# Quarter loads shared between two DMA queues, and two GpSimd products moved within a step, in an mLSTM cell followed by a leaky-ReLU feed-forward

## The chip, the cores and the metric

The kernel runs on one core of one Trainium2 chip. The metric is the device time of one execution in microseconds (us), taken as the median of several runs. A profile is taken of one further execution; its span counts from the first to the last instruction and is a little shorter than that execution's own time.

Engines are written as the profile writes them: PE (matrix multiplications; PEld is its weight load), DVE (VectorE), ACT (ScalarE), POOL (GpSimd) and SP (SyncE, which here only issues DMAs). SPq and ACTq are DMA issues by SP and by ACT. DVE, ACT, POOL and PE run their instructions in the order of the program.

## The reference

```python
# q, k, v, o_gate: (4, 8, 768, 40); i_gate, f_gate: (4, 8, 768), all float32
for t in range(S):
    m_new = np.maximum(f_gate[:, :, t] + m, i_gate[:, :, t])
    f_stab = np.exp(f_gate[:, :, t] + m - m_new)
    i_stab = np.exp(i_gate[:, :, t] - m_new)
    m = m_new
    C = f_stab[:, :, None, None] * C + i_stab[:, :, None, None] * np.einsum('bhd,bhe->bhde', vt, kt)
    n = f_stab[:, :, None] * n + i_stab[:, :, None] * kt
    h_tilde = np.einsum('bhde,bhe->bhd', C, qt)
    denom = np.maximum(np.abs(np.einsum('bhd,bhd->bh', n, qt)[:, :, None]), 1.0)
    y[:, :, t] = sigmoid(o_gate[:, :, t]) * h_tilde / denom
x = y.transpose(0, 2, 1, 3).reshape(3072, 320)
h = x @ w_in                                 # w_in: (320, 2048)
out = np.maximum(0.01 * h, h) @ w_out        # w_out: (2048, 320)
```

The two weight matrices arrive as 64-bit floats.

## The kernel before

**Steps and chunks.** The 768 tokens are cut into six chunks c of 128. A step s = 4c + b is one batch b's 128 tokens of chunk c with all eight heads, so there are 24 steps. Chunk 0 (steps 0 to 3) is written out by hand in `first_chunk`. From chunk 1 on a step works on two halves of 64 tokens and carries a state from half to half.

**The feed-forward beside it.** The loop at the end (L1319 on) runs, for each c from 1 to 6, the feed-forward of chunk c-1 as a row of `ffs` units, and puts the cell work of chunk c between the units. PE, DVE, ACT and POOL are filled by hand in this order; the list `place` says after which unit each cell unit comes in chunk 1. There the units are sixteen input products (`half`, L872, 256 columns of tokens each), then sixteen quarters of output products (`part`, L894). The cell units of chunk 1 are, for each step, `u_parts` then `u_plain`.

**A step of chunk 1.** `u_parts(s)` transposes the scaled q (`split_qs`, PE L623, copies on ACT L626), computes the scores inside each half (PE L725) and, mixed with them, the sums that carry the state (PE L731, from the decayed k and from v), multiplies the scores with the decays (DVE L742) and adds to the state (DVE L705, `state_add(s, 0)`). `u_plain(s)` multiplies the mixed q with the state and values (PE L785, tile hN), scales the state for the next half on POOL (L701, `state_next(s, 1)`), normalizes on DVE (L749 to L793), finishes x on POOL (L798, L799) and adds to the state (DVE L705, `state_add(s, 1)`).

**What is prepared ahead.** After `u_plain(s)` the loop calls `ahead(s + 1)`: transposes of k and q (PE L638, ACT L644), exponentials on ACT (L547), then on POOL the scaled q (`prep_qs`, L576, tile y), the state times its decay (`state_next(s+1, 0)`, L701), the decayed k (`prep_vu`, L567, tile vu, called `ku`), and the causal mask of the step after that (`prep_mask(s + 2)`, L537). Before `u_parts(s)` POOL also copies a step's v into place (`split_v`, L416). `ahead(4)` and `split_v(4)` to `split_v(7)` are called at units 3, 5, 9 and 11.

**The weights.** w_in is loaded in four quarters n of 512 columns. A quarter has a lower half r = 0 (256 columns, partitions 0 to 63) and an upper half r = 1 (256 columns, partitions 64 to 127); each of the two holds all 320 rows as five slots of 64. For the quarters 1 to 3 (`WHOLE`) the lower half is one DMA of 640 KB; the upper half is two, of 512 KB and 128 KB, because its slots are rotated (`SLOTS`). All three DMAs of a quarter are issued by SP, one after the other, with rows of 2048 bytes in 64 partitions. The 64-bit words land in a raw area and are narrowed to 32 bits by two ACT and four DVE instructions for each half e of a quarter (`narrow_weights`, L302 to L311), in the order set by `run(now, pace[i])`. The products of quarter n need its two halves e narrowed.

**The queues.** SP's DMAs keep the order in which the program calls `Ordered.dma_start` (L95) as long as `order["on"]` holds, that is through the first chunk and the list at L1283 to L1303: quarter 1 of w_in; the rewritten gates (L360) and the q of step 4; quarter 2; k, v and decays of step 4 (`feed`); quarter 3; then the loads of step 5 around the first part of w_out; steps 6 and 7 around the next parts. The q of step 6 follows behind the part of w_out at L1303. In the first 80 us ACT issues only five small loads of gates.

**The place of the loads.** In `first_chunk` ACT's program order around L1260 is: exponentials and copies of steps 2 and 3, `prep_o(2)` and `prep_o(3)` (ACT L583), then the activation of the next feed-forward unit (L880), the copies of x of steps 2 and 3 (L861, L862) and the narrowing of quarter 1 (`n0`, `n1`).

Of the kernel before, what the change touches and what calls it, by code (L numbers as in the profile page):

```python
# [18 lines left out]
def kernel(  # L19
# [26 lines left out]
    nc = tc.nc  # L46
    B, H, S, D = q.shape
# [3 lines left out]
    NS = B * NB  # L51
# [49 lines left out]
    sync, by_act = queues = Ordered(nc.sync), Ordered(nc.scalar)  # L101
# [20 lines left out]
    for u in range(2):  # L122
        part = ident[ts(u, SL), ts(u, SL)]
        nc.gpsimd.affine_select(
            part, part, compare_op=ALU.not_equal, fill=1.0, base=0, pattern=[[-1, SL]], channel_multiplier=1,
# [109 lines left out]

    WHOLE = (1, 2, 3)

    def load_weights(n, es=(0, 1)):

        m = n - QN  # L240
        if n < QN:
            dst = w_in[:, n, :]
        else:
            dst = w_out[:, 2 * m : 2 * m + 2, :].rearrange("p a d -> p (a d)")
        to = dst
        if wide:
            if n < 2:
                at = NF * GT - 2 * WC * (n + 1)
                raw = acts_l[:, at : at + 2 * WC].bitcast(U64)
            elif n < QN:  # L250
                raw = raw_t[:, WC * (n - 2) : WC * (n - 1)]
            elif m < 2:
                raw = w_out[:].rearrange("p f d -> p (f d)")[:, (2 + m) * WC : (3 + m) * WC].bitcast(U64)
            else:
                at = (4, 0, 1, 2, 3, 4)[m - 2] * HW
                raw = raw_t[:, at : at + HW]
            raws[n] = (raw, dst)
            to = raw
        if n < QN:
            src = moe_w_in[:, n * QC : (n + 1) * QC].rearrange("(k p) (r c) -> r p k c", p=DP, r=2)  # L260
            halves = to.rearrange("p (e k c) -> p e k c", e=2, k=KC)
            both = to.rearrange("p (k c) -> p k c", k=KC)
            if n in WHOLE:
                es = es[:1] if es[0] == 0 else ()
            for e in es:
                for r in range(2):
                    at = 0
                    while at < KC:
                        k0, n_k = run_of(r, at)
                        if n in WHOLE:  # L270
                            rows, part = both[DP * r : DP * (r + 1), at : at + n_k], src[r, :, k0 : k0 + n_k, :]
                        else:
                            rows, part = halves[DP * r : DP * (r + 1), e, at : at + n_k], src[r, :, k0 : k0 + n_k, ts(e, P)]
                        sync.dma_start(rows, part)
                        at += n_k
        else:
            rows = moe_w_out[2 * m * P : 2 * (m + 1) * P, :]
            sync.dma_start(to.rearrange("p (a d) -> p a d", d=Dm), rows.rearrange("(a p) d -> p a d", p=P))
# [270 lines left out]
    def prep_vu(s):  # L549

        c, b = divmod(s, B)
        d = st[s]
        if s < NS:
            d["vu"] = wk.tile([P, H, 2, V1], F32, name="vu")
            g = gT[c][:, 1, ts(b, H)].unsqueeze(2).unsqueeze(3)
            if c == 0:
                nc.gpsimd.tensor_tensor(
                    d["vu"][:, :, :, :DB], d["va"][:, :, :D].rearrange("p h (k d) -> p h k d", d=DB),
                    g.to_broadcast([P, H, 2, DB]), op=ALU.mult,
                )  # L560
                nc.gpsimd.tensor_tensor(
                    d["vu"][:, :, :, DB], d["va"][:, :, D : D + 2], gT[c][:, 1, ts(b, H)].unsqueeze(2).to_broadcast([P, H, 2]),
                    op=ALU.mult,
                )
            else:
                d["ku"] = d["vu"][:].rearrange("p h k d -> p (h k d)")[:, : H * D].rearrange("p (h d) -> p h d", d=D)
                nc.gpsimd.tensor_tensor(  # L567
                    d["ku"], d["k"][:, :, :D], gT[c][:, 1, ts(b, H)].unsqueeze(2).to_broadcast([P, H, D]), op=ALU.mult,
                )

    def prep_qs(s):

        c, b = divmod(s, B)
        d = st[s]
        d["qs"] = wk.tile([P, Dm], F32, name="y")[:].rearrange("p (h d) -> p h d", d=D)
        nc.gpsimd.tensor_tensor(  # L576
            d["qs"], natural(s, 1), gT[c][:, 2, ts(b, H)].unsqueeze(2).to_broadcast([P, H, D]), op=ALU.mult,
        )

    def prep_o(s):  # L580

        o = st[s]["o"] if s < B else natural(s, 2) if s < 2 * B else raw_blocks(s, 2, DB)
        nc.scalar.activation(o, o, AF.Tanh, scale=0.5)  # L583
# [169 lines left out]
    def u_values(s):  # L753
        d = st[s]
        pool, tag = (psc, "c") if s < 2 else (psf, "mm")
        pa = d["pa"] = pool.tile([P, H, D1], F32, name="pa", tag=tag)
        for h in range(H):
            for u in range(2):
                toks = ts(u, SL)
                nc.tensor.matmul(pa[toks, h, :], lhsT=d["w"][:, h, toks], rhs=d["va"][:, h, :D1], start=True, stop=True)  # L760
# [354 lines left out]
    def u_gates(c):  # L1115
        gates_T(c, bus.pop(c)[0])
# [67 lines left out]
    def first_chunk():  # L1184

        for n in range(2):
            for i in range(3):
                load_first(n, i)
        for n in range(2):
            load_first(n, 3)  # L1190
        load_weights(0, (0,))
        on_v, on_s = nc.vector.tensor_copy, nc.scalar.copy
        gates(0)
        gates_exp(0)
        load_fi(2)
        idle(3)
        ab = spread_masks()
        bu, a, _ = bus[0]
        a, left = replicate(a, bu)
        u_transpose(0, (on_v, on_v))  # L1200
        gates(1)
        spread_first(ab, a, left, 0)
        gates_T(0, bu)
        prep_vu(0)
        first_exps(ab, 0)
        u_scores(0)
        u_transpose(1, (on_s, on_s))
        prep_vu(1)
        prepare_tiles()
        u_values(0)  # L1210
        u_scores(1)
        ab = spread_masks()
        spread_first(ab, a, None, 2)
        e = next_exps(ab, 2)
        w, w1 = narrow_weights(0, 0), narrow_weights(0, 1)
        n0, n1 = narrow_weights(1, 0), narrow_weights(1, 1)
        prep_o(0)
        prep_o(1)
        gate(0)
        u_values(1)  # L1220
        load_first(2, 0)
        load_first(2, 1)
        load_weights(0, (1,))
        load_first(3, 0)
        load_first(3, 1)
        load_first(2, 2)
        load_first(3, 2)
        load_first(2, 3)
        load_first(3, 3)
        load_weights(1, (0,))  # L1230
        load_weights(1, (1,))
        run(e, 6)
        state(0)
        state(1)
        run(w, 2)
        u_x(0)
        gate(1)
        run(w, 4)
        u_x(1)
        state_copy(0)  # L1240
        state_copy(1)
        prepare_step(0)
        prepare_step(1)
        run(e, 2)
        ffs = ff_units(0)
        u_transpose(2, (on_s, on_s))
        run(e, 4)
        gates_exp(1)
        run(w1, 2)
        run(e, 4)  # L1250
        ffs[0]()
        run(w1, 2)
        prep_vu(2)
        prep_vu(3)
        u_scores(2)
        u_transpose(3, (on_v, on_s))
        run(w1, 2)
        u_gates(1)
        u_scores(3)
        prep_o(2)  # L1260
        prep_o(3)
        u_values(2)
        ffs[1]()
        gate(2)
        u_values(3)
        gate(3)
        u_x(2)
        state(2)
        u_x(3)
        state(3)  # L1270
        state_copy(2)
        run(n0, 4)
        state_copy(3)
        run(n0, 2)
        run(n1, 6)
        prepare_step(2)
        prepare_step(3)
        return ffs

    E = mybir.EngineType  # L1280
    with tc.manual_schedule(engines={E.PE, E.DVE, E.Activation, E.Pool}):
# [37 lines left out]
        for c in range(1, NB + 1):  # L1319
# [7 lines left out]
            def visits(i):  # L1327
                nonlocal done
                at = place if c == 1 else first_pairs if c == 2 else pairs
                while done < min(n_c, sum(p <= i for p in at)):  # L1330
                    fn, s = cells[done]
                    fn(s)
                    done += 1
                    if fn is u_mix:
                        waiting.append(s)
                    if fn is u_plain and s < 2 * B - 1 or fn is u_parts and s == 2 * B - 1:
                        ahead(s + 1)
                    elif fn is u_mix:
                        after.append(s + 2)
                    elif fn is u_plain:  # L1340
                        prep_mask(s + 2)
                        ahead(s + 2)

            for i in range(n_ff):
# [50 lines left out]
                while fed < done:  # L1395
                    fn, s = cells[fed]
# [42 lines left out]
```

## Time and profile before

| | us |
|---|---|
| median of 3 runs | 473.57 (472.79 to 474.94) |
| the profiled execution | 473.84 |
| its span | 472.0 |
| PE busy within the span | 463.1 |
| PE busy from 0 to 38 us | 33.97 of 38 |
| PE busy from 38 to 85 us | 45.02 of 47 |
| PE busy from 85 to 472 us | 384.08 of 387 |

The profile's timeline lists instructions by start (us from the span's start), duration, engine, line, operation, output and inputs; runs of the same instruction are merged with their count (x8). A bracket at the end tells the idle time of the engine before the instruction and what ended it. The list of waits has, for each pair of waiting and releasing work, us in total, how often, and the longest. The table of stretches gives for each stretch its length, the busy time of each engine with the number of instructions in it, the granted PE clock (1.00 everywhere), the mean busy share of the DMA engines and the rate that they moved.

From 0 to 38 us the kernel is the hand-written first chunk; from 38 to 85 us the input products of chunk 0 run beside steps 4, 5 and 6; from 85 us on one chunk follows the other. The DMA engines are above 90 % busy through most of the first 70 us (a mean share of 1.10 from 0 to 38 us and 0.93 from 38 to 85 us) and half busy after.

### The profile page before, as it was taken

The numbers are of one execution on the slowest core, as the hardware profiler recorded it, in microseconds if no ns is written. First come the engines' busy times: TensorE is split into PE (matmuls) and PEld (weight loads), VectorE is DVE, ScalarE is ACT, GpSimd is POOL, SyncE is SP. The second block draws the span as 40 slices with busy tenths as digits, with TensorE's granted clock in tenths as the row PEclk, the third lists the DMA queues.
The fourth block names the chain that finished last, engine by engine and source line by source line (L and its number), as shares of the span: only waits on it lengthen the run. The fifth ranks groups of instructions, "written<-read, shape, count | busy, mean of one in ns | idle before, by whom it ended". The sixth has DMA issues, their size and how long they took to land.

```text
span 472.0 us, 14167 instructions
## 1 busy us (share of the span) xinstructions
PE 463.1 (98%) x5716; PEld 416.3 (88%) x5716; DVE 336.8 (71%) x609; ACT 203.4 (43%) x497; POOL 171.7 (36%) x225
## 2 busy tenths in 40 slices
PE   9899999999999999999999999999999999999997
PEld 6677978777788999988999988999988999988997
DVE  5778688999479988867788867788847786104541
ACT  2657878755336511366311366311456311253210
POOL 4332377264335164923214923214822005300020
PEclk9999999999999999999999999999999999999999
DMA  9999998887732695865754865853875202100001
GB/s 130 169 192 187 188 205 220 206 181 145 153 110 65 159 166 112 176 153 129 171 119 106 181 130 126 198 114 79 188 151 124 74 9 81 58 0 2 8 8 42
DMA packets 160993, 59.21 MB, mean 125 GB/s; under 512 B 123808, under 2 KB 152352, under 8 KB 160928
## 3 DMA queue, kind: packets, MB, share of 16 engines
q1 hardware_dynamic: 120944, 51.15, 48.9%
q10 hardware_dynamic: 39984, 7.17, 9.4%
q8 instruction: 45, 0.74, 0.7%
q14 instruction: 20, 0.16, 0.1%
HBM read 51.58 MB, written 6.70 MB: 123 GB/s over the span
## 4 chain that ended last, share of the span: by engine, by line
PE 87%; SPq 5%; POOL 3%; issue 3%; DVE 1%; DMA 1%; ACT 0%; POOLq 0%
PE ph L1036 33%; PE po L929 33%; PE po L894 8%; SPq L95 5%; PE pT L813 3%; PE ph L872 3%; PE sd L725 3%; PE sd L731 1%; DMA raw<-in_o_gate_dram 1%; PE hN L785 1%; POOL w L537 1%; POOL y L576 1%; POOL S L701 1%; PE pa L760 0%; PE tk L638 0%
## 5 line engine op out<-in xcount | busy, mean ns | idle before, releaser
L929 PE MATMUL po<-w_out,acts 128*128 128x160 f32 x640 | 89.1, 300 | 0.0
L929 PEld LDWEIGHTS po<-w_out,acts 128*128 128x128 f32 x640 | 87.3, 190 | 0.6 <-ACT acts L1061 0.3
L1036 PE MATMUL ph<-xT,w_in 64*128 64x256 f32 x720 | 82.7, 378 | 0.0
L1036 PEld LDWEIGHTS ph<-xT,w_in 64*128 64x128 f32 x720 | 69.2, 187 | 8.6 <-issue 0.6
L1065 DVE TENSOR_TENSOR acts<-acts,ph 128x512 f32<-128x512 f32 x60 | 38.4, 683 | 40.7 <-PE ph L1036 40.6
L929 PE MATMUL po<-raw,acts 128*128 128x160 f32 x480 | 66.4, 300 | 0.0
L929 PEld LDWEIGHTS po<-raw,acts 128*128 128x128 f32 x480 | 65.4, 190 | 0.3
L537 POOL TENSOR_SCALAR_AFFINE_SELECT w<-w 64x512 f32<-64x512 f32 x40 | 34.0, 850 | 52.9 <-DMA w<-a_dr 51.7
L1069 ACT COPY acts<-ph 128x512 f32<-128x512 f32 x60 | 32.2, 588 | 48.8 <-PE ph L1036 48.8
L1061 ACT ACTIVATE acts<-acts 128x1024 f32<-128x1024 f32 x30 | 31.6, 1055 | 41.8 <-DVE acts L1065 32.4
L701 POOL TENSOR_TENSOR S<-S,f 40x336 f32<-40x336 f32 x36 | 30.6, 849 | 47.8 <-PE pT L813 32.1
L547 ACT ACTIVATE w<-w,gT 128x64 f32<-128x64 f32 x160 | 41.6, 337 | 11.7 <-DMA a_dr<-a 4.3
L742 DVE TENSOR_TENSOR qn<-w,sd 64x384 f32<-64x384 f32 (+1 forms) x80 | 33.4, 418 | 14.3 <-ACT acts L1069 8.4
L872 PE MATMUL ph<-xT,w_in 64*128 64x256 f32 x320 | 37.3, 381 | 0.9 <-issue 0.7
L894 PE MATMUL po<-w_out,acts 128*128 128x320 f32 x128 | 36.7, 437 | 0.0
L1036 PE MATMUL ph<-acts,w 64*128 64x256 f32 x320 | 36.3, 379 | 0.0
L827 POOL TENSOR_TENSOR xb<-xb,den 128x320 f32<-128x320 f32 x16 | 11.6, 727 | 67.0 <-DVE xb L824 64.7
L872 PEld LDWEIGHTS ph<-xT,w_in 64*128 64x128 f32 x320 | 31.9, 187 | 3.8 <-ACT w_out L303 0.9
L1036 PEld LDWEIGHTS ph<-acts,w 64*128 64x128 f32 x320 | 30.6, 187 | 3.6
L894 PEld LDWEIGHTS po<-w_out,acts 128*128 128x128 f32 x128 | 23.5, 190 | 9.2 <-ACT acts L880 0.3
L967 POOL TENSOR_TENSOR y<-y,raw 128x160 f32<-128x160 f32 x10 | 9.5, 950 | 59.5 <-ACT y L966 59.5
L612 DVE TENSOR_TENSOR qn<-kqT,ea 64x512 f32<-64x512 f32 x32 | 30.0, 939 | 0.8
(184 smaller groups left out, 732.2 us busy)
## 6 DMA issues: line engine op xcount, KB each, us to landing
rb<-in_k_dram SPq DMA_DIRECT2D x64, 80.0 KB
rb<-in_q_dram SPq DMA_DIRECT2D x64, 80.0 KB
rb<-in_o_gate_dram SPq DMA_DIRECT2D x64, 80.0 KB
ea<-a_dr SPq DMA_DIRECT2D x32, 128.0 KB
raw<-in_moe_w_out_dram SPq DMA_DIRECT2D x6, 640.0 KB
w<-a_dr ACTq DMA_DIRECT2D x24, 128.0 KB
x_dr<-x SPq DMA_DIRECT2D x64, 40.0 KB
xT<-x_dr SPq DMA_DIRECT2D x16, 160.0 KB
```

The source lines that it names most:

```text
L537: nc.gpsimd.affine_select(part, part, compare_op=ALU.is_ge, fill=-1e30, base=0, pattern=[[0, H], [1, SL]], channel_multiplier=-1,)
L547: yield nc.scalar.activation(w[:, h, :], w[:, h, :], AF.Exp, bias=gT[c][:, 0, bh : bh + 1], scale=1.0)
L612: nc.vector.tensor_tensor(mixed(s)[rows, 1 - r], d["kqT"][rows, 1].rearrange("p (h t) -> p h t", t=SL), d["ea"][rows], op=ALU.mult,)
L701: nc.gpsimd.tensor_tensor(new, old, g, op=ALU.mult)
L742: nc.vector.tensor_tensor(mixed(s)[toks, u, hs], w[toks, hs], bank[1 - u][to[u][hs.start], hs], op=ALU.mult,)
L872: nc.tensor.matmul(ph[r][:, cols], lhsT=w_row(r, slot, j), rhs=xT[DP * r : DP * (r + 1), slot, cols], start=(slot == 0), stop=(slot == KC ...
L894: nc.tensor.matmul(po[n][:], lhsT=acts[:, f, ts(n, P)], rhs=w_out[:, f, :], start=(f == 0), stop=(f == NF - 1),)
L929: nc.tensor.matmul(bank[:], lhsT=left[:, f, :], rhs=right[:, f, :], start=f == 0, stop=f == KH - 1)
L1036: nc.tensor.matmul(bank[r][:, e, :], lhsT=left(r)[rows, e], rhs=right(r)[rows], start=first and e == 0 and m == 0, stop=e == 1 and m == le ...
L1061: nc.scalar.activation(to, z, AF.Prelu, alpha=0.01)
L1065: nc.vector.tensor_tensor(to[:, 2 * r : 2 * r + 2], to[:, 2 * r : 2 * r + 2], bank[r], op=ALU.add)
L1069: nc.scalar.copy(to[:, 2 * r : 2 * r + 2], bank[r])
```

## The change

The change has two parts.

*Loads.* `load_weights` takes the halves r to load as `rs`. Without `rs`, quarters 1 to 3 load only their lower half, on SP as before. A new call in `first_chunk`, between `prep_o(3)` and `u_values(2)`, loads the upper halves of quarters 1, 2 and 3 by ACT's queue: six DMAs, two of each quarter, in this order. They are not part of SP's ordered list.

*GpSimd.* In `visits`, after `u_parts(s)` of steps 4, 5 and 6, `prep_qs(s + 1)` and `prep_vu(s + 1)` are called at once, so ahead of the POOL work of `u_plain(s)` and of `ahead(s + 1)`. The later calls in `ahead` find `qs` and `ku` there and do nothing. Step 4 itself, and steps from 8 on, are as before.

```diff
-    def load_weights(n, es=(0, 1)):
+    def load_weights(n, es=(0, 1), rs=None):
...
             for e in es:
-                for r in range(2):
+                for r in ((0,) if n in WHOLE else (0, 1)) if rs is None else rs:
                     at = 0
...
-                        sync.dma_start(rows, part)
+                        (sync if rs is None else nc.scalar).dma_start(rows, part)
                         at += n_k
...
         d = st[s]
-        if s < NS:
+        if s < NS and "ku" not in d:
             d["vu"] = wk.tile([P, H, 2, V1], F32, name="vu")
...
         d = st[s]
+        if "qs" in d:
+            return
         d["qs"] = wk.tile([P, Dm], F32, name="y")[:].rearrange("p (h d) -> p h d", d=D)
...
         prep_o(3)
+        for n in WHOLE:
+            load_weights(n, rs=(1,))
         u_values(2)
...
                     done += 1
+                    if fn is u_parts and s < 2 * B - 1:
+                        prep_qs(s + 1)
+                        prep_vu(s + 1)
                     if fn is u_mix:
```

## The prediction, made before the changed kernel was run

> **What bounds the kernel now.** I read the page's busy shares first, then the waits of PE, then the timelines of POOL, DVE, ACT and SP around the one wait that matters, and last the rates of the DMA engines.
>
> ```profile
> PE 463.1 (98%) x5716; PEld 416.3 (88%) x5716; DVE 336.8 (71%) x609; ACT 203.4 (43%) x497; POOL 171.7 (36%) x225
> ```
>
> PE is the bound: 8.9 us of a span of 472.0 are all that it ever waits. Of these, 4.0 lie before 38 us and 2.9 after 85 us, where the change alters little. That leaves 2.0 us between. PE's own waits from 38 us on are these:
>
> ```profile
> PE sd L731 <- POOL vu L567: 0.9, 1, 0.9
> PE ph L872 <- issue: 0.7, 1, 0.7
> PE dC L681 <- issue: 0.2, 1, 0.2
> ```
>
> One is named: PE, at the carried sums of step 5 (L731), waits 0.9 us for the decayed k from POOL. The timeline of POOL shows why it is late.
>
> ```profile
> 59.74 1.78 POOL L537 TENSOR_SCALAR_AFFINE_SELECT w<-w 64x512 f32<-64x512 f32 x2 [8.49 <-DMA w<-a_dr]
> 62.76 0.94 POOL L416 COPY S<-acts 64x320 f32<-64x320 f32 x2 [1.23 <-DMA acts<-in_v_dram]
> 63.77 0.76 POOL L701 TENSOR_TENSOR S<-S,f 40x336 f32<-40x336 f32 x1
> 64.61 0.72 POOL L798 TENSOR_TENSOR x<-x,den 128x320 f32<-128x320 f32 x1
> 65.40 0.71 POOL L799 COPY x<-x 128x64 f32<-128x64 f32 x1
> 66.07 1.39 POOL L576 TENSOR_TENSOR y<-rb,gT 128x320 f32<-128x320 f32 x1
> 67.54 0.90 POOL L701 TENSOR_TENSOR S<-S,f 40x336 f32<-40x336 f32 x1
> 68.51 0.85 POOL L567 TENSOR_TENSOR vu<-kn,gT 128x320 f32<-128x320 f32 x1
> ```
>
> POOL stands idle 8.49 us for the decays of step 5 and 1.23 us for its v; then its queue runs without a gap to the scaled q (L576) and the decayed k (L567). Both late transfers were issued by SP behind all of w_in:
>
> ```profile
> 36.10 6.61 SPq L95 DMA_DIRECT2D w<-a_dr  x2
> ...
> 43.39 2.84 SPq L95 DMA_DIRECT2D raw<-in_moe_w_in_dram  x3
> ...
> 47.89 6.71 SPq L95 DMA_DIRECT2D w_out<-in_moe_w_out_dram  x1
> 54.65 2.17 SPq L95 DMA_DIRECT2D w<-a_dr  x2
> ...
> 57.49 0.58 SPq L95 DMA_DIRECT2D acts<-in_v_dram  x1
> ```
>
> SP is held for 6.61 and 6.71 us in two issues whose like takes 0.6 (its queue is full), and so issues step 5's decays only at 54.65 and its v at 57.49.
>
> **Part 1, the loads.** Three upper halves of 655 KB leave SP's queue for ACT's. What that is worth depends on whether two queues move more than one. The rates of two stretches, the first almost wholly quarter 3 of w_in (64 partitions at a time), the second parts of w_out (128 partitions); the last columns are clock, DMA share and GB/s:
>
> ```profile
> 46.00:51.00 5.00, 4.29 (x65) 4.02 (x55) 4.73 (x10) 4.91 (x12) 4.62 (x6) 1.00 1.06 202
> 76.00:78.00 2.00, 2.00 (x76) 1.83 (x76) 1.90 (x6) 0.83 (x3) 1.48 (x2) 1.00 1.02 396
> ```
>
> With the DMA engines equally full, rows into 64 partitions move at 202 GB/s and rows into 128 at 396. An upper half is 655/202 = 3.2 us of this queue, three are 9.7. If lower and upper halves in flight together go at 396, everything that SP issues after quarter 3 lands up to 9.7 us sooner; if not, 0. I take half, 4.9 us, because part of the time the upper halves will run beside narrow rows of k and v instead of a lower half, and the row for that is missing.
>
> The DMA page of the Trainium skill (DMA: Bandwidth & Descriptors, Issuing engines are not separate DMA queues) speaks against it: all queues run on the same engines and interleave, and issuing from several engines saves only the issue time on the sequencer. By it the rate stays 202 and the first rival below decides; no run here has yet shown two full queues at once.
>
> On ACT the six issues stand where this row shows room, the idle time before the activation at 34.32:
>
> ```profile
> 34.32 0.66 ACT L880 ACTIVATE acts<-ph 128x256 f32<-128x256 f32 x2 [4.88 <-PE ph L872]
> ```
>
> ACT's own issues later in the trace take 0.45 to 0.66 us, at worst 1.30 (L1179). Six at 0.61 are 3.7 us: hidden in the 4.88. Six at 1.30 are 7.8: ACT would be free at 29.44 + 7.8 = 37.2 instead of 34.32; the activation (0.66) and the four copies of x (0.85 a pair) behind it then end at 39.6, and PE's product that needs the last copy starts there instead of at 38.49: +1.1 us. I take 0 (end for the range: +1.1). Quarter 1's upper half is asked for at about 29.5 instead of 26.3; its narrowing starts at 38.16. 655 KB at 202 GB/s is 3.2 us, shared with SP's queue 6.5: landed by 37 to 38, so 0, or +0.5 if it slips by 1 us, since the narrowed quarter was ready at 42.53 and used at 43.1.
>
> **Part 2, POOL.** For step 5 the two products, 1.39 + 0.85 us, go ahead of the state's scaling (L701 at 63.77). They need q, k and v of step 5 and nothing from PE, so they run as soon as split_v (L416) is done. With v landed 4.9 us sooner, at 57.9, POOL does L416 to 58.8, the scaled q to 60.3, the decayed k to 61.2, and L701 when PE's hN of step 4 is done (61.85): 61.9 to 62.7. PE arrives at the carried sums at 68.5 and finds all: **-0.9 us**. For step 6 the same two products come behind step 6's q, issued by SP at 69.84 today; sooner in the new queue, so 0. If it isn't, POOL's L701 after PE's hN of step 5 (76.14) ends 1.3 us later and the narrowing of w_out behind it on DVE (done 81.77, used by PE about 82.7) costs about +0.4, or +1.3 with PE 0.9 sooner. For step 7 POOL has 7.23 us idle before 91.06: 0.
>
> **What is late next.** DVE and PE behind the removed wait:
>
> ```profile
> 64.57 0.51 DVE L705 TENSOR_TENSOR S<-S,sd 40x336 f32<-40x336 f32 x1 [1.73 <-POOL S L701]
> ...
> 73.35 0.50 DVE L705 TENSOR_TENSOR S<-S,sd 40x336 f32<-40x336 f32 x1
> ```
>
> DVE waited 1.73 us for POOL's L701; that goes too. PE's hN of step 5 (74.92 today) needs the second L705 (done 73.85); PE will come at 74.0, DVE will be done about 72. No new wait there.
>
> **The sum.** 0 (ACT) + 0 (quarter 1) - 0.9 (step 5) + 0 (steps 6, 7) = -0.9 us on the profiled 473.84, so 472.9. That execution lies 0.27 above the median; on the median 473.57 this is **472.7**.
>
> **Rivals.**
>
> *Step 5's v is not sooner, and the moved products hold DVE.* If v still lands at 62.76, POOL does L416, 1.39 and 0.85, and only then L701, which ends at 66.9 instead of 64.5. DVE is in order: L705 waits 2.4 us, and behind it stand six instructions that narrow quarter 3, the scores of step 5 (L742) and its L705. DVE's only slack on the way is 0.34, so that L705 ends at 75.9; PE, at 74.0, waits 1.9. Net +1.0: **474.6**. It turns where v lands at 61.8 (1.0 us sooner: no change) and is gone at 60.9. For it: the rule above, and DMA shares above 1. Against it: 202 against 396 GB/s, and the 54.00 to 55.00 us stretch, in which the engines moved 26 GB/s because SP was held, which alone gives almost 1 us back.
>
> *ACT is held in its issues.* The trace's issue records go round eight semaphores that SP and ACT share, and an issue waits for the landing of the DMA eight before it (SP's v of step 4, at 34.50, waited for quarter 1's second DMA). ACT can so be bound to SP's transfers. At 1.30 each: -0.9 + 1.1 = 473.8. If one issue is held as SP's were, 6 us more: ACT is free at 39.1 instead of 33.1, the copies end at 41.5, PE loses 3.0: 475.7; with two held so, over 480. For it: ACT's queue never ran while SP's was this full. Against it: at 3 to 5 us ACT issued in 0.32 and 0.38 us while SP's issues took 0.76 to 1.18.
>
> *The wait only moves* (quarter 1 late by 1 us, or the narrowing of w_out for PE's 81.54 product): **473.6**, no change.
>
> *More than this goes.* The 0.7 us at 46.8, which the profile gives to no one, lies in the same stretch and might go as well: 472.0, with the small waits between 55 and 65 us (0.2) 471.8.
>
> **How the numbers follow.** Chances: forecast 0.55 (472.7); v not sooner 0.15 (474.6); ACT held 0.12 (473.8 to 475.7 and beyond); the wait moves 0.12 (473.6); more 0.06 (471.8). The predicted time is 472.7. Its own range, with 0.5 for the spread of a median (the three runs span 2.2 us), is 472.1 to 473.4. The range for 8 in 10 takes in the rivals but the far end of the second and the lowest of the last: **471.6 to 475.0**. Half a per cent is 2.4 us, about what a measurement of this kernel can tell from no change. PE's waits in reach sum to 2.0, so faster by over 2.4 needs a gain I don't see: 0.04. Slower by over 2.4 is ACT held in more than one issue, with a little of the first rival beyond its price: 0.10. Within: 0.86.
>
> **What would show it.** Right: no wait of PE at L731 in step 5; POOL's mask of step 5 before 57 us and its L416 before 60; L576 and L567 straight behind it; SP free of its two issues of over 6 us; rates near 400 GB/s between 30 and 45 us; ACT's activation near 34.3 unmoved. Wrong: rates that stay near 200 there, DVE's L705 waiting over 2 us for L701, PE waiting at hN L785; or ACT's activation and copies later than 35.5 and PE's product at 38.5 with them.

## The result, and the profile after

| | before | after |
|---|---|---|
| median, us | 474.25 (472.79 to 476.03, 4 runs) | **486.0** (483.95 to 486.58, 4 runs) |
| the profiled execution, us | 473.84 | 483.95 |
| its span, us | 472.0 | 482.2 |
| span's start to the first transposes of step 4 on PE, us | 45.33 | 57.20 |

The changed kernel is slower: the ratio of its times to those of the kernel before on the same chip is 1.0249, 95% interval 1.0216 to 1.0281. Behind L574 the lines of the changed kernel stand two further down: L861/862 is L863/864, L872 is L874, L880 is L882, L701 is L703, L705 is L707, L731 is L733, L785 is L787, L576 is L578; the loads are issued at L274 in both.

The page of the changed kernel, its span, the busy shares, and the granted PE clock in 40 slices of 12 us:

```profile
span 482.2 us, 14160 instructions
...
PE 463.2 (96%) x5716; PEld 414.9 (86%) x5716; DVE 335.1 (70%) x609; ACT 203.2 (42%) x497; POOL 170.8 (35%) x225
...
PEclk9996899999999999999999999999999999999999
```

PE is busy for as long as before (463.2 against 463.1 us); the span has grown by 10.2 us. So the work is the same and PE stands idle, and in the fourth and fifth slice (36 to 60 us) its clock is not full. The first line of the list of PE's waits says for what:

```profile
PE ph L874 <- ACT xT L863: 11.9, 1, 11.9
```

The wait of 0.9 us at the carried sums of step 5 (now L733) is gone from the list, and so is the 0.7 that had no name. In their place stands one wait of 11.9 us: the input products wait for ACT's copy of x. The timeline of PE shows where it lies, the timeline of ACT why:

```profile
35.90 0.51 PE L683 MATMUL dC<-vu,kn 128*40 128x42 f32 x16
48.34 8.93 PE L874 MATMUL ph<-xT,w_in 64*128 64x256 f32 x60 [11.94 <-ACT xT L863]
```

```profile
27.95 5.74 ACTq L274 DMA_DIRECT2D acts<-in_moe_w_in_dram  x2
...
38.10 8.44 ACTq L274 DMA_DIRECT2D raw<-in_moe_w_in_dram  x4
46.59 0.78 ACT L882 ACTIVATE acts<-ph 128x256 f32<-128x256 f32 x2 [18.18 <-DMA raw<-in_moe_w_in_dram]
47.26 0.37 ACT L863 COPY xT<-xt 128x256 f32<-128x256 f32 x1
```

From 28.4 us, when `prep_o(3)` ends, to 46.54 us ACT does nothing but issue the six loads. Its activation, at 34.32 before, starts at 46.59, and three of the four copies of x behind it are done at 48.3, when PE resumes. The chain of waits (start, us, what) names what held the last issue, back to the cause:

```profile
26.65 6.49 DMA a_dr<-a
...
33.20 4.49 SPq L95
...
37.74 0.59 SPq L95
...
38.38 7.64 DMA rb<-in_o_gate_dram
...
46.05 0.49 ACTq L274
...
46.59 0.38 ACT acts L882
```

ACT's last issue at 46.05 came when a load of the o gate had landed that SP had asked for at 38.38: a transfer that has nothing to do with the weights. The trace's records of the issues give for every DMA the semaphore that it reports to, and each of these issues itself carries a wait for that same semaphore, that is for the last DMA on it to have landed. For ACT's six:

```
issue at   what                       semaphore, its DMA before
27.95      quarter 1, 512 KB          102  SP's v of step 3 (landed 26.80)
33.16      quarter 1, 128 KB          107  SP's rewritten gates (issued 26.65, landed 33.14)
38.10      quarter 2, 512 KB          110  SP's lower half of quarter 2 (issued 27.70, landed 38.08)
38.80      quarter 2, 128 KB          102  ACT's own first load (issued 27.95, landed 38.72)
41.26      quarter 3, 512 KB          104  SP's v of step 4 (issued 29.38, landed 41.24)
46.05      quarter 3, 128 KB          108  SP's o gate (issued 38.38, landed 46.03)
```

Four of the six began 0.02 us after a landing of SP's, and one 0.08 us after one of ACT's own.

On SP and POOL what the change was to bring did come. SP's queue and then POOL:

```profile
33.20 5.13 SPq L95 DMA_DIRECT2D w<-a_dr  x2
...
44.60 6.77 SPq L95 DMA_DIRECT2D w_out<-in_moe_w_out_dram  x1
51.41 1.12 SPq L95 DMA_DIRECT2D w<-a_dr  x2
...
53.20 0.58 SPq L95 DMA_DIRECT2D acts<-in_v_dram  x1
```

```profile
56.93 2.13 POOL L537 TENSOR_SCALAR_AFFINE_SELECT w<-w 64x512 f32<-64x512 f32 x2 [10.64 <-DMA w<-a_dr]
59.21 1.82 POOL L416 COPY S<-acts 64x320 f32<-64x320 f32 x2 [0.15 <-DMA acts<-in_v_dram]
61.12 0.83 POOL L578 TENSOR_TENSOR y<-rb,gT 128x320 f32<-128x320 f32 x1
61.92 0.97 POOL L567 TENSOR_TENSOR vu<-kn,gT 128x320 f32<-128x320 f32 x1
```

Step 5's decays are asked for at 51.41 instead of 54.65 and its v at 53.20 instead of 57.49; POOL starts the mask at 56.93 instead of 59.74 and has the decayed k at 62.9 instead of 69.4. SP was still held twice, 5.13 and 6.77 us. What this was worth can't be read from the absent wait, though: PE starts the carried sums of step 5 at 78.83 us here and at 69.41 before, so that a decayed k as late as before would have been in time too.

**The account.** In the profile before, PE starts the transposes of step 4 (the first L638) at 45.33 us, and 426.7 us of span follow. In the one after it starts them (L640) at 57.20, and 425.0 follow. So 11.9 us were lost ahead of that point and 1.7 regained behind it; 11.9 - 1.7 is the 10.2 of the span. The 11.9 ahead are the wait of 11.94, plus 2.0 because the 60 products behind the wait took 8.93 instead of 6.91, less 2.1 because PE reached the wait sooner (36.41 against 38.56) in this execution, though it runs the same program up to there. The 60 products before:

```profile
38.49 6.91 PE L872 MATMUL ph<-xT,w_in 64*128 64x256 f32 x60
```

The 1.7 are not a gain of the change: a run below that moves neither a weight nor a product (the six loads of 3 KB) has 425.0 behind that point as well.

### The profile page after: what moved, and what is told of

Same layout as the page of the kernel before. It is cut to its first block, busy times and chain, and to the rows that moved or that the text cites. A ratio compares the mean times of both kernels' runs of the same rounds, so it can differ in the third digit from the quotient of the medians.

```text
span 482.2 us, 14160 instructions
## 1 busy us (share of the span) xinstructions
PE 463.2 (96%) x5716; PEld 414.9 (86%) x5716; DVE 335.1 (70%) x609; ACT 203.2 (42%) x497; POOL 170.8 (35%) x225
## 4 chain that ended last, share of the span: by engine, by line
PE 88%; DMA 4%; ACT 3%; SPq 2%; DVE 1%; issue 1%; POOL 0%; ACTq 0%; DVEq 0%; POOLq 0%
PE ph L1038 33%; PE po L931 32%; PE po L896 7%; PE ph L874 4%; PE pT L815 3%; PE sd L727 3%; SPq L95 2%; DMA rb<-in_o_gate_dram 2%; DMA a_dr<-a 1%; DMA rb<-in_k_dram 1%; PE sd L733 1%; PE hN L787 1%; PE ab L508 1%; PE ab L492 1%; ACT w L526 1%
## 5 line engine op out<-in xcount | busy, mean ns | idle before, releaser
L1038 PE MATMUL ph<-xT,w_in 64*128 64x256 f32 x720 | 82.7, 378 | 0.0
L1067 DVE TENSOR_TENSOR acts<-acts,ph 128x512 f32<-128x512 f32 x60 | 38.4, 683 | 40.7 <-PE ph L1038 40.6
L703 POOL TENSOR_TENSOR S<-S,f 40x336 f32<-40x336 f32 x36 | 31.5, 876 | 59.2 <-PE pT L815 33.1
L537 POOL TENSOR_SCALAR_AFFINE_SELECT w<-w 64x512 f32<-64x512 f32 x40 | 32.9, 823 | 54.8 <-DMA w<-a_dr 53.3
L874 PE MATMUL ph<-xT,w_in 64*128 64x256 f32 x320 | 39.4, 398 | 12.6 <-ACT xT L863 11.9
L874 PEld LDWEIGHTS ph<-xT,w_in 64*128 64x128 f32 x320 | 32.3, 197 | 17.3 <-ACT xT L863 12.1
```

Of the source, the lines that this page charges most:

```text
L537: nc.gpsimd.affine_select(part, part, compare_op=ALU.is_ge, fill=-1e30, base=0, pattern=[[0, H], [1, SL]], channel_multiplier=-1,)
L703: nc.gpsimd.tensor_tensor(new, old, g, op=ALU.mult)
L874: nc.tensor.matmul(ph[r][:, cols], lhsT=w_row(r, slot, j), rhs=xT[DP * r : DP * (r + 1), slot, cols], start=(slot == 0), stop=(slot == KC ...
L1038: nc.tensor.matmul(bank[r][:, e, :], lhsT=left(r)[rows, e], rhs=right(r)[rows], start=first and e == 0 and m == 0, stop=e == 1 and m == le ...
L1067: nc.vector.tensor_tensor(to[:, 2 * r : 2 * r + 2], to[:, 2 * r : 2 * r + 2], bank[r], op=ALU.add)
```

## The experiments

The theory, **shared semaphores**: ACT's issues wait on semaphores that SP uses too, for a DMA of SP's some places earlier, whatever ACT itself loads. Its rivals: **the bytes** (the loads in two queues come no sooner, and quarter 1 comes later), and **POOL's part**, priced in the prediction as its first rival. On top, **the clock**: behind an idle time PE runs at half speed for some us. Where an expectation says S, it is the shared semaphores.

### POOL's part alone

All loads on SP as before; the moved products as in the change. Against the kernel before:

```diff
-        if s < NS:
+        if s < NS and "ku" not in d:
...
+        if "qs" in d:
+            return
...
+                    if fn is u_parts and s < 2 * B - 1:
+                        prep_qs(s + 1)
+                        prep_vu(s + 1)
```

> Only the GpSimd part: the scaled q and decayed k of steps 5, 6 and 7 go ahead of the state's scaling, and all of w_in stays on SP's queue. Theory A (the moved products are free and take PE's 0.9 us wait for the decayed k away): 0.9 us faster than before, no wait of PE at the carried sums of step 5. Theory B (without earlier transfers they hold the state's scaling and with it DVE): POOL's scaling L701 of step 4 ends near 66.9 us instead of 64.5, DVE's L705 waits about 4 us for it instead of 1.7, PE waits near 1.9 us at hN of step 5, 1.0 us slower than before. In neither case does it come near the 11 us that the whole change lost.

Measured: 475.54 us (474.02 to 476.9, 12 runs), ratio 1.0022 (1.0002 to 1.0042), so +1.0 us (0.1 to 2.0; the medians on that chip differ by 1.6). The timelines of DVE, then of PE (waits of hN and of the first output products):

```profile
65.30 0.51 DVE L707 TENSOR_TENSOR S<-S,sd 40x336 f32<-40x336 f32 x1 [3.59 <-POOL S L703]
...
73.43 0.50 DVE L707 TENSOR_TENSOR S<-S,sd 40x336 f32<-40x336 f32 x1
```

```profile
74.08 1.10 PE L787 MATMUL hN<-S,qn 128*64 128x42 f32 x30 [1.03 <-ACT acts L882]
83.53 1.34 PE L896 MATMUL po<-w_out,acts 128*128 128x320 f32 x4 [1.53 <-DVE w_out L311]
```

With v still at 62 us, the two products stand ahead of the state's scaling, DVE's addition waits 3.59 us instead of 1.73, and hN waits 1.0 until the addition of step 5 is done at 73.93 (the profile names ACT, whose activation ends at 74.08 too). The wait at L733 is gone (0.9), so that these two nearly cancel: from step 4's transposes to step 6's it takes 31.0 us here and 30.7 before. The step 6 products wait 2.99 us for q and push the narrowing of w_out, so that PE waits 1.5 there, which is most of the loss. Alone, the part costs more than it saves.

### The loads alone

The change without the calls of `prep_qs` and `prep_vu` behind `u_parts`.

```diff
-                    if fn is u_parts and s < 2 * B - 1:
-                        prep_qs(s + 1)
-                        prep_vu(s + 1)
```

> Only the loads: the upper halves of quarters 1 to 3 on ACT's queue, POOL's order as before. If the loss is all of the loads: 10 to 12 us slower than before, ACT in its six issues until about 46.5 us, PE waiting near 12 us for ACT's copies of x. If the two parts make the loss together: less than 6 us.

Measured: 485.84 us (485.12 to 486.49, 4 runs), ratio 1.0250 (1.0226 to 1.0275). ACT:

```profile
35.77 12.57 ACTq L274 DMA_DIRECT2D raw<-in_moe_w_in_dram  x4
48.39 0.76 ACT L882 ACTIVATE acts<-ph 128x256 f32<-128x256 f32 x2 [18.50 <-DMA rb<-in_o_gate_dram]
```

All of the loss is the loads'. Behind the start of step 4's transposes 424.9 us of span follow, as after the whole change (425.0), though no product was moved. ACT is held to 48.4 here, 1.8 us longer than in the profile after; the profiled execution after was the shortest of its four, which fits.

### Only quarter 1's two loads on ACT

```diff
-                for r in ((0,) if n in WHOLE else (0, 1)) if rs is None else rs:
+                for r in ((0,) if n == 1 else (0, 1)) if rs is None else rs:
...
-        for n in WHOLE:
-            load_weights(n, rs=(1,))
+        load_weights(1, rs=(1,))
...
-                    if fn is u_parts and s < 2 * B - 1:
-                        prep_qs(s + 1)
-                        prep_vu(s + 1)
```

(Quarters 2 and 3 whole on SP; no change on POOL.)

> Of the loads only quarter 1's two DMAs on ACT; quarters 2 and 3 whole on SP, POOL's order as before. Theory S (an issue waits for the landing of the DMA that had the same one of eight shared semaphores before it): ACT's second issue waits for the lower half of quarter 2, landed near 34 to 36 us, so ACT is free at about 35 to 36, PE loses at most 1 us, total within 1.5 us of before. Theory Q (ACT's issues are held as long as the DMA engines are full): they are full until 54 us with or without the other four DMAs, so each issue takes 3 us or more and ACT is free after 34 only if two issues are so much less than six; PE loses 0 to 4 us.

Measured: 483.1 us (481.76 to 483.76, 4 runs), ratio 1.0189 (1.0163 to 1.0215). The expectation was missed by far. ACT:

```profile
29.13 10.42 ACTq L274 DMA_DIRECT2D acts<-in_moe_w_in_dram  x2
39.60 0.66 ACT L882 ACTIVATE acts<-ph 128x256 f32<-128x256 f32 x2 [10.00 <-DMA raw<-in_moe_w_in_dram]
...
46.58 0.78 ACT L302 ACTIVATE w_in<-acts 128x640 f32<-128x640 f32 x1 [5.01 <-DMA acts<-in_moe_w_in_dram]
```

The second issue fell on semaphore 110, whose last DMA was quarter 2's lower half, and stood until 39.05. So the shared semaphores named the right DMA, but it landed 3 us or more later than expected. The 128 KB that it asked for came only at 46.5, so the narrowing of quarter 1 was late as well, and PE waited twice for long: 4.0 us for ACT, and 3.8 for DVE's state copies, which stand behind the narrowing in DVE's order. Two issues are enough, if one of them meets a semaphore in use.

### Six loads of 3 KB in all

The kernel before, with six DMAs of 32 x 16 bytes that nothing reads, issued by ACT where the change puts its six.

```diff
+    small = gp.tile([BH, 6, 4], F32, name="small")
...
         prep_o(3)
+        for n in range(6):
+            nc.scalar.dma_start(small[:, n, :], f_all[:, :4])
         u_values(2)
```

> The kernel before with w_in wholly on SP and six loads of 32 x 16 bytes added on ACT's queue at the place of the changed kernel's loads; nobody reads them. Theory S: the size is of no matter, the six wait in turn for SP's DMAs eight before them, the last for the k of step 4, which lands near 42 us: ACT in its issues until about 42, PE waits 6 to 7 us for ACT's copies of x, 6 to 8 us slower than before. Theory Q (what held ACT is the 1.9 MB in a full queue): 3 KB change nothing, six issues at 0.4 us end near 32, within 0.5 us of before.

Measured: 481.39 us (481.35 to 481.77, 4 runs), ratio 1.0159 (1.0133 to 1.0186), +7.5 us, within the 6 to 8 expected. ACT and PE (lines one further down than in the kernel before):

```profile
34.69 9.95 ACTq L1264 DMA_DIRECT2D small<-in_f_gate_dram  x6
44.69 0.76 ACT L881 ACTIVATE acts<-ph 128x256 f32<-128x256 f32 x2 [14.33 <-DMA small<-in_f_gate_dram]
```

```profile
45.22 0.79 PE L682 MATMUL dC<-vu,kn 128*40 128x42 f32 x16 [6.56 <-ACT acts L881]
...
54.57 0.25 PE L639 MATMUL tk<-ident,kn 64*40 64x64 f32 x2
```

In the records of the issues the six stood at 34.69, 35.41, 36.15, 40.22, 42.99 and 44.33 us, on semaphores whose last DMAs were quarter 1's, the rewritten gates', quarter 2's and k's of step 4, all SP's; each began 0.02 us after that DMA had landed. No weight moved queues, 3 KB more were transferred, and ACT was idle for 14.33 us where it was for 4.88 before. That decides for the shared semaphores and against the bytes.

PE starts step 4's transposes at 54.57, and 425.0 us of the span of 479.6 follow, 1.7 fewer than before, as in the profile after. Here no load of the kernel and no product was moved, so the 1.7 there are no gain of the change. The likely reason, not tested, is that PE comes 9 us later and finds the loads of steps 4 and 5 landed.

### The loads on a third queue

The changed kernel with the same six loads issued by GpSimd. In the trace they report to six semaphores that no other DMA uses, and the issues carry no wait.

```diff
-                        (sync if rs is None else nc.scalar).dma_start(rows, part)
+                        (sync if rs is None else nc.gpsimd).dma_start(rows, part)
```

> The changed kernel with the six loads of the upper halves issued by GpSimd instead of ACT, at the same place. GpSimd's loads count on eight semaphores of their own, unused until then, so no issue waits. Theory S (all of the loss is ACT held by the semaphores that it shares with SP): ACT's activation is back near 33 us, PE's 11.9 us wait is gone, the total is within 2 us of before; if v of step 5 then lands before 61 us, the 0.9 us wait goes too and it is about 473. Theory Q (two full queues cost as such: narrow rows of k and v crawl beside wide ones): k or v of step 4 lands after 45 us, PE waits at the transposes L640 or L872 products of quarter 1, 2 us or more slower than before although ACT is free.

Measured: 476.81 us (476.05 to 478.86, 6 runs), ratio 1.0069 (1.0046 to 1.0092). ACT, then PE:

```profile
34.58 0.66 ACT L882 ACTIVATE acts<-ph 128x256 f32<-128x256 f32 x2 [4.51 <-PE ph L874]
...
40.79 0.79 ACT L302 ACTIVATE w_in<-acts 128x640 f32<-128x640 f32 x1 [2.30 <-DMA acts<-in_moe_w_in_dram]
```

```profile
38.84 2.85 PE L874 MATMUL ph<-xT,w_in 64*128 64x256 f32 x22
43.48 6.24 PE L874 MATMUL ph<-xT,w_in 64*128 64x256 f32 x38 [1.79 <-DVE S L691]
```

The same bytes in another queue, without the shared semaphores, and ACT's activation stands at 34.58, as before the change: 9.2 of the 11.75 us of the loss (medians) go. The 3.3 us that are left by the ratio miss the 2 us of the expectation. They are a wait of 1.8 us, because quarter 1's upper half now shares the rate with quarters 2 and 3, its narrowing starts at 40.79 instead of 38.16, and DVE's state copies (L691) stand behind it; and slower products behind that wait (38 in 6.24 us; at 6.91 for 60 they would take 4.4). In that theory Q was right: the loads cost something with ACT free, too, and k of step 4 landed at 47.4 instead of 43.7, though PE did not wait for it. The rate itself, in the stretch from 30 to 46 us, before and here (last columns clock, DMA share, GB/s):

```profile
30.00:46.00 16.00, 15.36 (x250) 13.44 (x251) 12.76 (x32) 8.41 (x19) 2.78 (x7) 1.00 1.13 193
```

```profile
30.00:46.00 16.00, 13.47 (x181) 11.45 (x182) 10.56 (x28) 5.68 (x13) 4.12 (x10) 0.94 1.12 208
```

193 against 208 GB/s (208 in the profile after, too): with a second queue the same stretch moves 8% more, not twice as much.

### Only quarters 2 and 3 on the third queue

As the run above, but quarter 1 whole on SP, and the call for the other two behind `state_copy(3)`. That was meant to put them behind GpSimd's zero fills.

```diff
-                for r in ((0,) if n in WHOLE else (0, 1)) if rs is None else rs:
+                for r in ((0,) if n in (2, 3) else (0, 1)) if rs is None else rs:
...
-                        (sync if rs is None else nc.scalar).dma_start(rows, part)
+                        (sync if rs is None else nc.gpsimd).dma_start(rows, part)
...
-        for n in WHOLE:
-            load_weights(n, rs=(1,))
...
         run(n0, 4)
         state_copy(3)
+        for n in (2, 3):
+            load_weights(n, rs=(1,))
         run(n0, 2)
```

> The changed kernel with the upper halves of quarters 2 and 3 issued by GpSimd behind its zero fills of the states (about 36.5 us), and quarter 1 whole on SP as before. Theory: what was left of the loss with a third queue (3.3 us: PE waited 1.8 for quarter 1's narrowing, and its next 38 products took 6.24 instead of 4.4) came from quarter 1's halves sharing the rate with the two others; here quarter 1 lands as before, so ACT's first narrowing starts near 38, PE has no wait over 1 us at L874, clock 1.00: 472.7 to 474.0. Rival: the three queues still share some 205 GB/s, so that what is asked for sooner makes k and decays of step 4 later; PE waits there and the time is 474.5 or more.

Measured: 475.39 us (473.35 to 477.21, 12 runs), ratio 1.0028 (1.0008 to 1.0048). The loads were not issued at 36.5 us: the zero fills come with `prepare_step`, behind the new call, and GpSimd issued all four as early as in the run above:

```profile
28.49 2.47 POOL L274 DMA_DIRECT2D raw<-in_moe_w_in_dram  x4
```

So the run tests quarter 1 whole on SP, and not a later request. Quarter 1 came as before (narrowing from 38.30) and the clock stayed at 1.00. PE's largest waits:

```profile
PE po L896 <- DVE w_out L311: 1.3, 1, 1.3
PE tk L640 <- DMA kn<-in_k_dram: 1.2, 1, 1.2
```

The rival held: what the one queue gains the other loses. Step 4's k came late (landed at 47.0 instead of 43.7), and with v of step 5 copied at 61.3 PE waits for the narrowing of w_out as in the run of POOL's part alone.

### Fillers in the wait

The changed kernel with matrix products on PE that nothing reads, in the place of the wait: 44 of them, then 90.

```diff
         state(3)
+        spare = st[3]["pa"][:].rearrange("p h d -> p (h d)")[:, : 2 * P].rearrange("p (n t) -> p n t", t=P)
+        for _ in range(44):
+            nc.tensor.matmul(spare, lhsT=blank, rhs=blank.unsqueeze(1).to_broadcast([P, 2, P]), start=True, stop=True)
         state_copy(2)
```

> The changed kernel with 44 matmuls of 128x256 bf16 on PE put where PE waits for ACT's copies of x; they write a PSUM area that is read already, and nobody reads what they write. They should take about 10 us and lie wholly within the wait of 11.9 us. Theory C (PE's granted clock is taken down because PE idles, 0.55 on average from 38 to 50 us, and the products after it run slower, 8.9 us for 60 where before had 6.9): the clock stays at 1.00, the 60 products take 6.9 us, and the loss against before falls from 11.7 us to between 9 and 10. Theory N (the clock has another reason, or the slower products are hidden): the loss stays at 11.7 or grows by what the matmuls overrun.

> The changed kernel with 90 filler products on PE behind the last state sums of step 3 (44 took 4.98 us in the run with 44, so 90 take about 10.2, the length of the wait). They do no part of the computation. Theory H (an idle PE lowers its own granted clock for some us after it resumes): no idle of PE over 1 us between 36 and 51 us, granted clock 1.00 through 60 us, the 60 input products behind take 6.9 us instead of 8.9 (after) or 9.8 (with 44 fillers, which left 5.3 us idle); time about 484, 2 us under the changed kernel. Rival: the clock falls for another reason (the transfers, or ACT's and DVE's load at that time), the 60 products take about 9 again, time 486 or more.

Measured: with 44, 485.83 us (484.16 to 487.45, 4 runs), ratio 1.0251 (1.0224 to 1.0279); with 90, 485.28 us (484.73 to 486.08, 4 runs), ratio 1.0242 (1.0217 to 1.0268). PE with 44, then with 90:

```profile
40.36 4.98 PE L1277 MATMUL pa<-acts 128*128 128x256 bf16 x44
50.63 9.80 PE L874 MATMUL ph<-xT,w_in 64*128 64x256 f32 x60 [5.29 <-ACT xT L863]
```

```profile
38.29 10.00 PE L1277 MATMUL pa<-acts 128*128 128x256 bf16 x90
50.46 2.43 PE L874 MATMUL ph<-xT,w_in 64*128 64x256 f32 x20 [2.17 <-ACT xT L863]
53.39 4.59 PE L874 MATMUL ph<-xT,w_in 64*128 64x256 f32 x40 [0.50 <-DVE S L691]
```

The 44 took half of the 10 us expected and left 5.3 us idle, and the 60 products took 9.80. With 90 an idle time of 2.2 us was left, but the clock was 1.00 in every half microsecond from 46 to 56 us, and 20 and 40 products took 2.43 and 4.59, 7.02 together. The transfers went on (201 GB/s from 38 to 50 us). The other executions agree: the mean clock over the span was 0.982 to 0.986 in the four of the changed kernel, 0.989 to 0.996 in the four with 44 fillers, and 1.000 in three of the four with 90 (0.993 in the fourth). So the clock is lost by PE's idle time, not by the transfers. For the time the expectation of about 484 was not met. From ACT's activation to the transposes of step 4 there are 10.6 us in the profile after, 10.4 in that of the loads alone, 11.5 with 44 and 9.2 with 90 fillers, so 1.2 to 2.3 us were gained there; but the medians, 486.0 and 485.28, have overlapping intervals and don't tell that gain from nothing.

### Three smaller ways to the same wait

On the kernel before: the decayed k ahead of the state's scaling in `ahead` for steps below 8; the first part of w_out asked for behind step 5's loads; both.

```diff
+            if s < 2 * B:
+                prep_vu(s)
             state_next(s, 0)
-            prep_vu(s)
+            if s >= 2 * B:
+                prep_vu(s)
```

```diff
-        load_weights(QN + 0)
         feed(5, (2,))
         load_late(5, 1)
         feed(5, (1,))
+        load_weights(QN + 0)
```

> The kernel before with one pair exchanged in `ahead`: for steps 5, 6 and 7 the decayed k goes on POOL in front of the state's scaling of the same step, not in front of anything of the step before. Theory (PE's 0.9 us wait for the decayed k is all that POOL's order costs, and DVE's L705 of step 4 isn't touched): the decayed k is done 0.9 us sooner, the wait falls to 0.1 or less, 0.9 us faster than before. Rival (the next wait takes it, DVE's narrowing of w_out before the first output product, as in the run with the products alone): PE waits at L894 instead, no change.

> The kernel before with the first part of w_out asked for behind step 5's decays, q, v and k instead of ahead of its decays, on SP as ever. Theory: step 5's v is late because 640 KB of w_out (3.2 us at 202 GB/s) stand ahead of it, so its v lands 2 to 3 us sooner, POOL copies it before 61 us, the wait at L731 of 0.9 us goes: 472.7 to 473.2. Rival: SP stands as long in the issue of the decays as it stood in w_out's (6.7 us), so v comes under 1.5 us sooner and the time is 473.5, no change.

> Both edits to the kernel before: the decayed k of steps 4 to 7 ahead of the state's scaling on POOL, and the first part of w_out behind step 5's loads. Theory: each removes the same wait of 0.9 us at step 5, so together no more than one of them: 472.5 to 473.0, and no PE wait at L731. Rival: the earlier k makes the state's scaling on POOL late for DVE's second half of the state (L705), which without the sooner v waited 4.2 us; with it under 2, so that a few tenths more go: 472.2.

Measured: k first 473.03 us (472.06 to 476.42, 12 runs), ratio 0.9991 (0.9971 to 1.0011); w_out later 473.29 (472.37 to 475.55, 12 runs), 0.9997 (0.9979 to 1.0016); both 473.23 (471.87 to 479.24, 12 runs), 1.0002 (0.9974 to 1.0030, without the run of 479.24). In the first, the list of PE's waits still has a rest, beside waits of 2.2 and 0.9 us for q and k at transposes (L638):

```profile
PE sd L731 <- POOL vu L567: 0.2, 1, 0.2
```

In the second the wait is gone; SP and POOL:

```profile
47.33 6.97 SPq L95 DMA_DIRECT2D w<-a_dr  x2
54.34 0.59 SPq L95 DMA_DIRECT2D rb<-in_q_dram  x1
54.97 0.58 SPq L95 DMA_DIRECT2D acts<-in_v_dram  x1
```

```profile
58.60 0.94 POOL L416 COPY S<-acts 64x320 f32<-64x320 f32 x2 [0.37 <-DMA acts<-in_v_dram]
```

SP was held 6.97 us in the decays' issue as it had been in that of w_out, yet v was copied at 58.60 instead of 62.76. In this profile 425.0 us of span follow the start of step 4's transposes, 1.7 fewer than before, and here PE is not late (45.58 against 45.33). But this execution was the shortest of its twelve, and no median shows the gain: all three intervals hold 1. No version run here is shown to be faster than the kernel before.

## Why the prediction was wrong

**The step that failed** is "On ACT the six issues stand where this row shows room", with "Six at 0.61 are 3.7 us: hidden in the 4.88" and its far end of +1.1. It priced an issue by the duration of ACT's issues late in the trace. The time was not in the duration but in the wait ahead of it, for the landing of an earlier DMA: ACT was done at 46.54 instead of the 33.1 forecast, or 37.2 at the far end, and PE lost 11.9 us. The six issues themselves took 0.49 to 1.78 us each, 4.8 together, so the size was nearly right and the term was the wrong one. The zero for quarter 1 was too small as well: its upper half landed at 38.7 and 40.7 instead of 37 to 38. In the changed kernel ACT's hold hid that; with ACT free, on the third queue, it cost the wait of 1.8.

**The second rival was the answer and was priced too low.** "ACT is held in its issues" named the eight semaphores, gave SP's v of step 4 as an example, and wrote "with two held so, over 480". It got 0.12, and the range ended at 475.0, short of one held issue (475.7). Its counter-argument was the two short ACT issues at 3 to 5 us. But the second of these, at 4.38, began 0.02 us after SP's k on the same semaphore had landed: it was a case of the rival, and short only because the duration leaves the wait out. The profile before had what was needed. SP's own k and v of step 4, at 31.88 and 34.50, each began 0.07 us after the landing of the DMA before on their semaphore, and those two had taken 6.9 and 8.2 us from issue to landing. Four of six ACT issues waited for a DMA of SP's.

The price of a held issue, 6 us, was taken from something else: SP's 6.61 and 6.71 us lie within the issues, whose semaphores were free 0.7 and 2.6 us earlier. What held SP there, a full queue as the prediction has it or another thing, was not tried; none of ACT's six issues took that long.

**The rate** was taken half-way between 202 and 396 GB/s. Measured are 193 before and 208 with a third queue, so lower and upper halves in flight together do not go at 396; that number belongs to the parts of w_out, and what makes them quicker was not tried. The Trainium skill (DMA: Bandwidth & Descriptors, Issuing engines are not separate DMA queues) says that DMAs of several engines run on the same DMA engines and that only the sequencer's issue time is saved. The trace agrees on the rate; on the issue time the runs here show a cost in place of a saving, since ACT stood idle for 14.33 us over loads of 3 KB.

**The gain**, -0.9 at step 5 with the 0.7 without a name as the last rival, is not shown. Both waits went, 1.7 in the account of the profile, but they went with six loads of 3 KB that nobody reads, too. v was asked for 4.3 us sooner (4.9 forecast), but not by the rate that was to bring it: three upper halves fewer stood ahead of it on SP, and part is the earlier first chunk of that execution. POOL's products ran straight behind L416 as forecast. The nearest to the gain by itself is the run with w_out later, 1.7 in its profile and nothing that its median can tell.

**The first rival** was right where its condition holds, in the run of POOL's part alone: +1.0 forecast, +1.0 measured. That the sums agree is luck in part: it foresaw L703 ending at 66.9 and a wait at hN of 1.9; these were 65.3 and 1.0, which alone would be nearly nothing, and the w_out narrowing, priced at up to +1.3 in another place, came to 1.5.

**What was to show it wrong** did: ACT's activation and copies later than 35.5 and PE's product at 38.5 with them, and a rate that stayed near 200 (207 GB/s from 30 to 45 us).

## What to carry to other kernels

Before a DMA is moved to an engine that also computes, list the DMAs in flight at that moment by the semaphores that they report to: the issue can stand until the DMA that used its semaphore last has landed, and everything behind it in that engine's order stands too. How long is told by the time from issue to landing in that stretch (6.5 to 11.9 us for the four DMAs of SP's here), and not by the durations of the issues, which leave the wait out. A queue with semaphores of its own took away most of this loss, but it shares the same rate and was still slower than the kernel before (1.0069); nor was any order within the one queue that was tried here shown to gain.

Before a wait that is gone is booked as a gain, look whether the waiting engine simply came later. Here the six loads of 3 KB, which can gain nothing, showed the same 1.7 us.

## What was not expected of the hardware

**The clock falls while PE idles.** In the profile after, the granted clock fell to 0.50 about 2.8 us after PE went idle (36.4 to 39.2) and came back 4.5 us after it resumed (48.34 to 52.8). The windows of the two stretches (last columns clock, DMA share, GB/s):

```profile
38.00:50.00 12.00, 1.66 (x8) 1.40 (x10) 0.60 (x2) 3.40 (x9) 4.41 (x7) 0.55 1.10 205
50.00:60.00 10.00, 10.00 (x134) 8.36 (x134) 9.31 (x20) 6.68 (x15) 2.85 (x3) 0.86 1.17 212
```

So a long wait costs more than its length: the 60 products behind it, 6.91 us before, took 8.22 (six loads of 3 KB) to 9.80 (44 fillers). The Trainium skill (TensorE: Matmul & The Clock Gate, Part 1: The HAM clock gate) states half speed after an idle window of about 3.4 us and full speed after as long a busy one; the traces agree on the half, but here the fall came sooner, after 2.8 us. The stretches at half clock in the traces' clock records last 3.41 us (third queue), 6.83 (quarter 1, twice; six loads of 3 KB; 44 fillers) or 13.65 (after; the loads alone): one, two or four times the same length. Which idle time starts one was not tried. In the third queue's run 1.8 us were enough, while 2.2 us in the run with 90 fillers brought none; and in the last of the three smaller runs an idle time of 1.0 us, ended at 28.2, was followed by a stretch of 6.83 from 29.2, while the same idle time in the profile before was followed by none.

**A small load can be slow.** In the run of quarter 1 alone, 128 KB issued at 39.05 landed at 46.5 us, while SP's transfers filled the DMA engines (a mean share of 1.09 from 39 to 46.5 us). Of the six loads of 512 bytes the first, issued at 34.69, landed at 43.5 (a share of 1.05 from 34 to 46 us).
